# Attention, feed-forward and gate in one kernel: exponentials without a bias pointer, a new opening, new shares between ScalarE and VectorE, last sums in halves

## The chip, the cores and the metric

The kernel runs on one core of a Trainium2 chip. Its engines are TensorE (PE, matmuls; PEld are its weight loads), VectorE (DVE), ScalarE (ACT), GpSimd (POOL) and SyncE (SP, which mostly issues DMAs). The metric is the device time of one execution in microseconds. Executions of one kernel mostly agree within about 0.5%. Ratios are the mean time of one kernel's runs over the mean time of the other's runs in the same rounds, so they are not quite the ratios of the medians quoted beside them.

## The reference, cut to what matters

```python
B, S, D = 1, 2048, 640 ; H = 32 ; Dh = 20 ; F = 1536          # x, weights bfloat16
# A: attention without a mask
qkv = split(x @ wqkv)                       # per head q, k, v: 2048 x 20
p   = softmax(q @ k.T * Dh ** -0.5)         # 32 heads x 2048 x 2048 exponentials
a   = concat(p @ v) @ wo
# B: feed-forward with mish
h   = x @ w1 + b1
b   = (h * tanh(log1p(exp(h)))) @ w2
g   = sigmoid((x * gate_w).sum(-1))
out = g * a + (1 - g) * b
```

There are 134 million exponentials. ScalarE looks them up. The kernel gives a part of them to VectorE, which builds the bits of an approximate exponential by arithmetic.

## The kernel before

The work is cut into 32 groups G: four heads (one of eight sets `p`) by 512 queries. In a group there are 16 key tiles of 128 keys. Each key tile goes to ScalarE or to VectorE.

- ScalarE's key tiles: TensorE fills S0 or S1 (two banks of PSUM each) with the scores of two heads, 128 keys by 2 x 512 queries. One ScalarE instruction makes the exponentials of 128x1024 into an exp buffer E in SBUF. Two of these are one key tile for four heads.
- VectorE's key tiles: scores go to D. VectorE converts them to 16-bit integers that are the bits of a bfloat16 exponential (t0), and makes two shifted copies (t1, t2). The sum of the three is the approximation, too large by the constant 3.1187. So ScalarE's exponentials were made too large by the same constant, through the bias ln(3.1187), and the normalisation takes it out of both.
- X is one more bank, for the projections and the feed-forward.
- TensorE multiplies the buffers by the values into C, one single bank of PSUM. A group's sums must be complete, and copied from C by VectorE (`oraw`), before the next group may start in C. Until then the exp buffers of the next group can't be freed. There are six.

A scheduler written into the kernel, in Python, decides the order of every engine's instructions before the program is built. It goes by a cost that each task is given, and by starting points (`at(...)`, in groups) of the projections and of the feed-forward stages, which are fitted between the attention's work. It also inserts junk matmuls ("filler", line 378 of before) into TensorE's expected gaps, to hold its clock.

```python
DVE_KEYS = (1, 4, 7, 10, 13, 14)
MISH_IN = (4, 10, 11, 17, 24, 25)
def dve_keys(G):                       # VectorE's key tiles of group G: 152 of 512 in all
    if G == 0:
        return DVE_KEYS[2:5]
    return DVE_KEYS[:6 if G in MISH_IN else 4 + G % 2]
# ...
        def ex(sb=sb, eb=eb, w=w):     # ScalarE: exponentials of two heads
            eb.tile = epool.tile([P, 2 * QC], BF16, tag="E", name="E")
            nc.scalar.activation(eb.tile[:, 0:w * QC], sb.tile[:, 0:w * QC], ACT.Exp, bias=lnc, scale=inv)
        te.__init__("ACT", 143 + 0.833 * w * QC, ex, [ts, prev], ...)      # cost told to the scheduler, ns
# ...
            def p1(xb=xb, hp=hp):      # VectorE: the bits of the exponentials
                nc.vector.tensor_scalar(out=bufs[0].tile[...], in0=xb.tile,
                    scalar1=P * LOG2E * inv, scalar2=127.0 * P, op0=ALU.mult, op1=ALU.add)
# ...
    for c in range(NQ):                # the feed-forward's starting points
        base = 0.9 + 6.6 * c
        for ft in range(FT):
            h_unit(c, ft, at(base + 2.8 * ft / FT), base)
        mish(c, base + 3.1)            # Exp, Ln, Tanh on ScalarE, 128x2048 from SBUF to SBUF
```

The softmax here doesn't subtract the row's maximum and nothing guards it: scores larger than these inputs give would overflow.

Of the kernel before, what the change touches and what calls it, by code (L numbers as in the profile page):

```python
# [10 lines left out]
P = 128  # L11
# [25 lines left out]

def dve_keys(G):
    if G == 0:
        return DVE_KEYS[2:5]  # L40
    return DVE_KEYS[:6 if G in MISH_IN else 4 + G % 2]

# [7 lines left out]
MISH_IN = (4, 10, 11, 17, 24, 25)  # L50
# [8 lines left out]
class Task:  # L59
    def __init__(self, eng, cost, fn, deps=(), after=None, prio=5, rings=(),  # L60
                 frees=(), lat=70, mode=None, rows=(), key=0, port=False, work=0):
        self.eng, self.cost, self.fn = eng, cost, fn
        self.deps, self.after, self.prio = [d for d in deps if d], after, prio
        self.rings, self.frees = list(rings), list(frees)
        self.lat, self.mode, self.rows, self.key, self.port = lat, mode, rows, key, port
        self.start = self.end = self.before = None

        self.work = work or {"row": 128 * len(rows), "col": 2.4 * cost - 15, "full": 2.2 * cost}.get(mode, 0)


class Ring:
    def __init__(self, n):
        self.free = deque((0.0, s) for s in range(n))

# [9 lines left out]
class Order:  # L84
# [4 lines left out]
    LOW = 2  # L89
    WARM = 0.55  # L90
# [38 lines left out]
    def pick_pe(self, c):  # L129
# [19 lines left out]
        if X and X[1].due + 14 < self.visit:  # L149
            lim = min(lim, X[0])  # L150
            over = min(over, lim + self.OVER)
        ok = []
        for e, t in rest:
            if self.units and t.rings and t.rings[0].unit:
                continue
            if e <= now + 1 and e + self.cost(t) <= over and lim > now + 1:
                ok.append((e, t))
        if ok:
            short = self.spare and len(self.spare.free) < self.LOW
            return min(ok, key=lambda x: (  # L160
                x[1].prio - (1.2 if x[1].mode == self.mode else 0)
                - (1 if short and x[1].prio == 2 else 0), x[1].key, x[1].n))
# [39 lines left out]
    def run(self):  # L202
# [16 lines left out]
        while left:  # L219
# [42 lines left out]
            for b in t.rings:  # L262
                b.slot = b.ring.free.popleft()[1]
            for b in t.frees:
                b.users -= 1
                b.last = max(b.last, t.end)
                if b.users == 0:
                    b.ring.free = deque(sorted(list(b.ring.free) + [(b.last, b.slot)]))
                    if b.unit:
                        self.units -= 1  # L270
# [16 lines left out]
def kernel(  # L287
# [35 lines left out]
    pair = const.tile([P, 2], F32, tag="pair")  # L323
    lnc, mask = pair[:, 0:1], pair[:, 1:2]
    oc = const.tile([P, NQ * 4 * QC], BF16, tag="oc")
    bs = const.tile([P, 3 * NU * D], BF16, tag="bs")
    arena = const.tile([P, 2 * FT * QC], BF16, tag="arena")
# [20 lines left out]
    def bs_of(c):  # L348
# [5 lines left out]
    epool = ctx.enter_context(tc.tile_pool(name="epool", bufs=6))  # L354
# [8 lines left out]
    R = {k: Ring(n) for k, n in (  # L363
        ("S0", 1), ("S1", 1), ("X", 1), ("D", 1), ("E", 6), ("T0", TB[0]), ("T1", TB[1]), ("T2", TB[2]),
# [26 lines left out]

    nc.vector.memset(gw, 0.0)
    nc.vector.memset(lnc, log(SUM))
# [15 lines left out]
    ld_x = {0: [load_x(nc.scalar, 0, 2, 4000), load_x(nc.sync, 2, 4, 4000)]}  # L409
# [22 lines left out]
    def warm():  # L432
        junk.tile = pt(junk)
        for i in range(20):
            nc.tensor.matmul(junk.tile[:, 0:P], lhsT=ident, rhs=ident, start=True, stop=True)
    t_warm = o.add("PE", 2500, warm, [t_ident], prio=1.05, mode="full", rings=[junk], frees=[junk])
# [4 lines left out]
    for c in range(4):  # L441
        for i, kts in enumerate(((0, 1), (2, 3), (4,))):
            w = len(kts)
            buf = Buf(R[("D", "S0", "S1")[i] if c == 0 else "XD"[(c + i) % 2]])
# [9 lines left out]
            on_act = c == 0 and i == 1  # L454

            def ev(c=c, kts=kts, buf=buf, on_act=on_act):
                dst = xt[:, c, kts[0]:kts[0] + len(kts), :]
                src = buf.tile[:, 0:512 * len(kts)].rearrange("p (k q) -> p k q", q=QC)
                if on_act:
                    nc.scalar.copy(out=dst, in_=src)  # L460
                else:
                    nc.vector.tensor_copy(out=dst, in_=src)
            t_xt[c, i] = o.add("ACT" if on_act else "DVE",
                               160 + 0.833 * 512 * w if on_act else from_psum(512 * w, 0.52),
                               ev, [t], prio=1, key=c, frees=[buf])
    xt_of = lambda c: [t_xt[c, 0], t_xt[c, 1], t_xt[c, 2]]


    def unit(n, cost, mm, evac, ev_cost, deps, after, key, prio=3, ev_prio=2, eng="DVE", takes=(),
             ev_deps=(), ev_frees=(), mode="col", ring="X"):  # L470
# [3 lines left out]
        for k in range(n):  # L474
            def fn(k=k):
                if k == 0:
# [4 lines left out]
                         rings=[buf] if k == 0 else [], mode=mode, key=key)  # L481
        return o.add(eng, ev_cost, lambda: evac(buf.tile), [prev] + list(ev_deps), prio=ev_prio, key=key,
# [19 lines left out]
    first_of = {}  # L502
    for n, blk in enumerate(passes):
        for r, G, j in blk:
            first_of.setdefault(G, n)
    first_of[NG] = len(passes)
# [11 lines left out]
    def k_unit(p, sc, after, prio=3, key=0, ring="X"):  # L518
        if sc == 0:
            k_buf[p] = Buf(R["K"])  # L520

        def mm(t, k):
            for r in range(4):
                c = (4 * p + r) * DH
                w = w0[:, 1, k, r * DH:r * DH + 32] if p == 0 else wqk[:, k, D + c:D + c + 32]
                nc.tensor.matmul(t[32 * r:32 * r + 32, 0:QC], lhsT=w, rhs=xt[:, sc, k, :],  # L526
                                 start=k == 0, stop=k == KT - 1, tile_position=(0, 32 * r))
        t_k[p, sc] = unit(
            KT, 219, mm,
            lambda t: nc.vector.tensor_scalar(  # L530
                out=kt[:, (p % 2) * S + sc * QC:(p % 2) * S + (sc + 1) * QC], in0=t[:, 0:QC],
                scalar1=mask, scalar2=None, op0=ALU.mult),
            746, xt_of(sc) + [ld_w0[1] if p == 0 else ld_wqk], after, key, prio,
            takes=[k_buf[p]] if sc == 0 else [], ring=ring)

    def q_unit(G, after, prio=3, key=0, ring="X"):
# [10 lines left out]
        def evac(t):  # L547
# [3 lines left out]
            else:  # L551
# [3 lines left out]
                      ring=ring)  # L555
# [30 lines left out]
    k_unit(0, 0, None, prio=1.1)  # L586
    q_unit(0, None, prio=1.1, ring="D")
# [54 lines left out]
    for p, a, z in ((1, 0.7, 2.8), (2, 4.0, 5.2), (3, 10.2, 11.2), (4, 12.6, 15.0), (5, 17.2, 18.4),  # L642
                    (6, 20.4, 23.0), (7, 24.1, 25.2)):
        for sc in range(4):
            k_unit(p, sc, at(a + (z - a) * sc / 4), prio=2.5, key=a + (z - a) * sc / 4)
    for b, a in ((1, 4.0), (2, 10.6), (3, 17.2)):
# [3 lines left out]
    t_sel = o.add("POOL", 2000, make_sel, [t_k[7, sc] for sc in range(4)], prio=2)  # L650
# [7 lines left out]
    def pv_four(G, items, term=0):  # L658
# [4 lines left out]
        def fn():  # L663
# [3 lines left out]
            for r, (j, _, buf, off) in enumerate(items):  # L667
# [5 lines left out]
                                 rhs=buf.tile.bitcast(BF16)[:, off * QC:(off + 1) * QC],  # L673
# [17 lines left out]
    for n, blk in enumerate(passes):  # L691
# [8 lines left out]
        deps = [t_q[G] for _, G, _ in blk] + [t_k[G // NQ, j // 4] for _, G, j in blk] + [ps]  # L700
# [6 lines left out]
        def ex(sb=sb, eb=eb, w=w):  # L707
            eb.tile = epool.tile([P, 2 * QC], BF16, tag="E", name="E")
            nc.scalar.activation(eb.tile[:, 0:w * QC], sb.tile[:, 0:w * QC], ACT.Exp, bias=lnc, scale=inv)  # L709

        te = marks[n]
        te.__init__("ACT", 143 + 0.833 * w * QC, ex, [ts, prev], prio=2, key=n, rings=[eb], frees=[sb])
# [10 lines left out]
    def d_batch(key):  # L723
# [6 lines left out]
        for hp in range(2):  # L730
# [6 lines left out]
            d = o.add("PE", 228, dfill, [go, t_q[G], t_k[G // NQ, j // 4]], prio=1, rings=[xb], mode="row",  # L737
# [3 lines left out]
            def p1(xb=xb, hp=hp):  # L741
                if bufs[0].tile is None:
# [3 lines left out]
                    scalar1=P * LOG2E * inv, scalar2=127.0 * P, op0=ALU.mult, op1=ALU.add)  # L746
# [32 lines left out]
    for G in range(NG):  # L779
# [7 lines left out]
        last = G == NG - 1  # L787

        def evac(G=G, ob=ob):
            ob.tile = opool.tile([P, QC], F32, tag="oraw", name="oraw")  # L790
            nc.vector.tensor_copy(out=ob.tile, in_=acc[G])  # L791
        t0 = o.add("DVE", from_psum(QC), evac, pv_done[G], prio=0, key=G, rings=[ob])

        if last:

            def spread_pe(ob=ob, den=den):
                den["p"] = psum.tile([P, QC], F32, tag="C", name="Cd")
                nc.tensor.matmul(den["p"][:, :], lhsT=sel, rhs=ob.tile, start=True, stop=True)
            t1 = o.add("PE", 900, spread_pe, [t0, t_sel], prio=1.5, key=G, mode="full")

            def inverse(rb=rb, den=den):
                rb.tile = opool.tile([P, QC], F32, tag="rbc", name="rbc")
                nc.scalar.activation(rb.tile, den["p"], ACT.Ln)
                nc.scalar.activation(rb.tile, rb.tile, ACT.Exp, scale=-1.0)
            o.add("ACT", 1300, lambda: nc.scalar.preload_act_table_set("natural_log_exp_and_others"),
                  [prev], prio=1, key=G)
            t4 = o.add("ACT", 1180, inverse, [t1], prio=2, key=G, rings=[rb])
# [4 lines left out]
        if not last:  # L812
            t1 = o.add("SP", 2200, gather, [t0], prio=0, key=G)
# [4 lines left out]
        if not last:  # L818
            t2 = o.add("DVE", 245, rec, [t1], prio=2, key=G)
# [4 lines left out]
        if not last:  # L824
            t3 = o.add("SP", 2200, spread, [t2], prio=0, key=G)
# [5 lines left out]
        if not last:  # L831
            t4 = o.add("SP", 3000, bcast, [t3], prio=0, key=G, rings=[rb])
# [38 lines left out]
    def mish(c, group):  # L871

        done = []
        for i, func in enumerate((ACT.Exp, ACT.Ln, ACT.Tanh)):
            now = []
            for a in range(3):
# [11 lines left out]
                now.append(o.add("ACT", 1930 + (1300 if i and a == 0 else 0), fn, deps,  # L888
# [49 lines left out]

    def f_pair(c, u, ring, after):
# [3 lines left out]
        for k in range(6):  # L943
            for hf in range(2):
# [5 lines left out]
                prev = o.add("PE", 138, fn, deps + ([t_on[4 * NP - 4 + c][1]] if k == 5 else []), after=after,  # L950
# [8 lines left out]
    for c in range(NQ):  # L959
        base = 0.9 + 6.6 * c  # L960
        for ft in range(FT):
            h_unit(c, ft, at(base + 2.8 * ft / FT), base)
        mish(c, base + 3.1)
        for u in range(NU):
            for hf in range(2):
                b_unit(c, u, hf, at(base + 4.6 + 2.0 * (2 * u + hf) / 8), base + 4)
    PAIRS = ((2, ("D",) * 4, 32), (3, ("S0", "S1", "D", "S0"), 32))
    for c in range(2):
        for u in range(NU):
            for hf in range(2):  # L970
                f_unit(c, u, hf, at(29.3 + c + 0.6 * (2 * u + hf) / 8), 29 + c)
# [35 lines left out]
```

## Time and profile before

The median was 856.27 us (855.61 to 856.63).

| ScalarE before | us |
|---|---|
| span of the profiled run | 857.3 |
| busy | 812.7 |
| start of the first exponential | 12.5 |
| idle between the first and the last | 19.8 |
| from the end of the last to the end | 17.7 |

The first two lines are the busy time of each engine from the page, with its share of the span and the number of instructions, and ScalarE's row of the 40 slices (tenths of busy time).

```profile
PE 819.6 (96%) x10778; PEld 299.5 (35%) x10778; DVE 737.9 (86%) x981; ACT 812.7 (95%) x771; POOL 7.0 (1%) x10
...
ACT  4888999999999999999999999999999989999992
```

ScalarE is full nearly everywhere; TensorE looks as full, but its record counts modelled ends and filler. The next lines are groups of instructions of before: line, engine, operation, what it writes and reads, shapes, count, then busy time in us and mean duration in ns, then idle time before it and who ended most of it.

```profile
L709 ACT ACTIVATE E<-S,pair 128x1024 bf16<-128x1024 f32 x720 | 734.8, 1138 | 20.0 <-PE C L670 10.9
L744 DVE TENSOR_SCALAR t<-D 128x1024 uint16<-128x1024 f32 x304 | 371.2, 1221 | 58.6 <-PE D L683 52.1
...
L881 ACT ACTIVATE arena<-arena 128x2048 bf16<-128x2048 bf16 x36 | 69.1, 1927 | 0.2
...
L378 PE MATMUL C<-xt,gw 128*32 128x512 bf16 (+6 forms) x476 | 35.1, 361 | 0.0
```

720 exponentials of 1138 ns would be 819 us, but their busy time is 735: neighbours overlap. So a duration is not what one more costs; the distance from start to start is. The table of windows, for the exponentials alone (length of the stretch, busy time, count, granted clock, DMA share, GB/s), shows a full stretch:

```profile
518.00:614.00 96.00, 95.73 (x96) 1.00 0.06 17
```

For activations without a pointer there are the feed-forward's, three of 128x2048 in a row, in the chain of waits of before (start, length, what):

```profile
681.19 5.51 ACT arena L881 x3
```

Last, who kept ScalarE waiting before (total us, times, longest):

```profile
ACT E L709 <- PE C L670: 10.9, 8, 3.1
ACT E L709 <- PE S L683: 5.2, 8, 2.7
```

This profile is of an execution that took 859.09 us, 2.8 more than the median. Its clock record has half clock from 690.0 to 696.8 us, and ScalarE is idle for 2.3 us between 690 and 697. So some of the 19.8 us of idle time may belong to this execution and not to the kernel.

### The profile page before, as it was taken

The page shows a single profiled execution, that of the slowest core. Times are in us where ns is not written, and L with a number is a line of the kernel's source. Part 1 is how long each engine was busy: PE and PEld are TensorE (multiplying, and loading weights), DVE is VectorE, ACT ScalarE, POOL GpSimd, SP SyncE. Part 2 cuts the span into 40 slices and gives each one's busy share as a digit, 9 for nine tenths or more (in the row PEclk, how much of TensorE's full clock was granted, in tenths as well). Part 3 has the DMA queues.
Part 4 walks back from the last instruction along what each step waited for, and adds up shares of the span by engine and source line. Part 5 has one row for each costly group of instructions (what it writes and reads, how often), then busy time and mean ns, then how long its engine had stood idle before and what let it go on. Part 6 is the DMA issues. An engine that isn't in the chain of part 4 may idle for free.

```text
span 857.3 us, 24774 instructions
## 1 busy us (share of the span) xinstructions
PE 819.6 (96%) x10778; PEld 299.5 (35%) x10778; DVE 737.9 (86%) x981; ACT 812.7 (95%) x771; POOL 7.0 (1%) x10
## 2 busy tenths in 40 slices
PE   8999999899999998999999999999999999999998
PEld 5422234333323343333322333333223333333335
DVE  3699999998889999999898978889898988978984
ACT  4888999999999999999999999999999989999992
POOL 2000000000000000000000000000000000000000
PEclk9999999999999999999999999999999989999999
DMA  9510000000000000000000000000000000000112
GB/s 320 152 17 17 12 12 19 15 15 11 19 18 18 18 15 5 19 19 19 19 19 18 15 5 18 18 16 18 19 6 18 19 2 19 19 19 23 37 38 72
DMA packets 32244, 25.23 MB, mean 29 GB/s; under 512 B 17731, under 2 KB 26883, under 8 KB 32135
## 3 DMA queue, kind: packets, MB, share of 16 engines
q1 hardware_dynamic: 30678, 22.55, 9.2%
q8 instruction: 84, 1.38, 0.7%
q10 hardware_dynamic: 1456, 1.10, 0.4%
q14 instruction: 26, 0.20, 0.1%
HBM read 18.20 MB, written 2.88 MB: 25 GB/s over the span
## 4 chain that ended last, share of the span: by engine, by line
PE 54%; ACT 30%; issue 9%; DVE 5%; DMA 2%; SPq 0%; DVEq 0%; ACTq 0%
ACT E L709 26%; PE S L683 16%; PE C L670 14%; PE X L488 11%; PE D L683 4%; ACT arena L881 3%; DVE t L744 3%; PE X L526 3%; PE X L544 2%; PE X L564 1%; PE D L488 1%; PE C L378 1%; DMA rows<-rec 1%; PE S L488 1%; DMA rbc<-rows 1%
## 5 line engine op out<-in xcount | busy, mean ns | idle before, releaser
L709 ACT ACTIVATE E<-S,pair 128x1024 bf16<-128x1024 f32 x720 | 734.8, 1138 | 20.0 <-PE C L670 10.9
L744 DVE TENSOR_SCALAR t<-D 128x1024 uint16<-128x1024 f32 x304 | 371.2, 1221 | 58.6 <-PE D L683 52.1
L683 PE MATMUL S<-q,kt 32*128 32x512 bf16 x1440 | 279.3, 383 | 18.3 <-ACT E L709 14.4
L758 DVE TENSOR_SCALAR t<-t 128x2048 uint16<-128x2048 uint16 x304 | 199.9, 682 | 1.4 <-PE C L670 0.3
L683 PEld LDWEIGHTS <-kt 32*128 32x128 bf16 x2048 | 91.5, 91 | 289.3 <-issue 276.5
L670 PE MATMUL C<-E,va 128*32 128x512 bf16 x1440 | 142.4, 388 | 1.4 <-DVE oraw L791 1.3
L683 PE MATMUL D<-q,kt 32*128 32x512 bf16 x608 | 118.1, 383 | 6.7 <-DVE t L744 5.3
L670 PE MATMUL C<-t,vs 128*32 128x512 bf16 x1216 | 112.6, 384 | 1.0 <-DVE t L758 1.0
L670 PEld LDWEIGHTS <-va 128*32 128x32 bf16 x2048 | 54.5, 95 | 85.9 <-issue 71.6
L488 PE MATMUL X<-w,arena 128*32 128x320 bf16 x1536 | 80.4, 306 | 0.0
L488 PE MATMUL X<-xt,w 128*32 128x512 bf16 x960 | 73.7, 383 | 1.0 <-DVE arena L867 0.7
L881 ACT ACTIVATE arena<-arena 128x2048 bf16<-128x2048 bf16 x36 | 69.1, 1927 | 0.2
L670 PE MATMUL C<-t,va 128*32 128x512 bf16 x608 | 61.7, 383 | 1.0 <-DVE oraw L791 0.5
L488 PEld LDWEIGHTS <-arena 128*32 128x32 bf16 x1536 | 33.9, 96 | 35.6 <-issue 27.7
L670 PEld LDWEIGHTS <-vs 128*32 128x32 bf16 x1216 | 31.3, 95 | 36.6 <-issue 27.6
L544 PE MATMUL X<-xt,wqk 128*32 128x512 bf16 x560 | 42.5, 382 | 0.0
L526 PE MATMUL X<-xt,wqk 128*32 128x512 bf16 x560 | 41.5, 382 | 0.0
L867 DVE TENSOR_SCALAR arena<-X,b 128x512 bf16<-128x512 f32 x48 | 35.7, 743 | 3.0 <-PE X L488 2.8
L378 PE MATMUL C<-xt,gw 128*32 128x512 bf16 (+6 forms) x476 | 35.1, 361 | 0.0
L488 PEld LDWEIGHTS <-w 128*32 128x32 bf16 x960 | 21.2, 95 | 30.4 <-issue 22.5
L564 PE MATMUL X<-wvt,xt 128*128 128x160 bf16 x310 | 28.3, 233 | 1.4 <-DVE kt L530 0.7
L530 DVE TENSOR_SCALAR kt<-X,pair 128x512 bf16<-128x512 f32 x30 | 22.4, 746 | 8.3 <-PE X L526 8.2
(82 smaller groups left out, 335.3 us busy)
## 6 DMA issues: line engine op xcount, KB each, us to landing
rbc<-rows SPq DMA_DIRECT2D x124, 64.0 KB
w<-in_B_w_dram SPq DMA_DIRECT2D x2, 1920.0 KB
out_dram<-arena SPq DMA_DIRECT2D x16, 160.0 KB
oc<-on SPq DMA_DIRECT2D x96, 20.0 KB
wqk<-in_A_wqkv_dram SPq DMA_DIRECT2D x1, 1600.0 KB
arena<-in_A_x_dram SPq DMA_DIRECT2D x2, 640.0 KB
wvt<-in_A_wqkv_dram SPq DMA_DIRECT2D x1, 800.0 KB
arena<-in_A_x_dram ACTq DMA_DIRECT2D x1, 640.0 KB
```

The source lines that it names most:

```text
L378: nc.tensor.matmul(t[32 * r:32 * r + 32, 0:n], lhsT=gw[:, 0, 1:33], rhs=xt[:, r, 0, 0:n], start=G is None, stop=G is None, tile_position=( ...
L488: nc.tensor.matmul(t[32 * r:32 * r + 32, 0:width], lhsT=lhsT(r), rhs=rhs, start=a, stop=b, tile_position=(0, 32 * r))
L526: nc.tensor.matmul(t[32 * r:32 * r + 32, 0:QC], lhsT=w, rhs=xt[:, sc, k, :], start=k == 0, stop=k == KT - 1, tile_position=(0, 32 * r))
L544: nc.tensor.matmul(t[32 * r:32 * r + 32, 0:QC], lhsT=w, rhs=xt[:, qc, k, :], start=k == 0, stop=k == KT - 1, tile_position=(0, 32 * r))
L564: nc.tensor.matmul(t[:, n * 160:(n + 1) * 160], lhsT=xt[:, js[n] // 4, k, (js[n] % 4) * P:(js[n] % 4 + 1) * P], rhs=wv[:, k, 160 * b:160 * ...
L670: nc.tensor.matmul(acc[G][32 * r:32 * r + 32, :], lhsT=vs4[:, b, term - 1, DVE_KEYS.index(j), h:h + 32] if term else va4[:, b, j, h:h + 32 ...
L683: nc.tensor.matmul(t[:, off * QC:(off + 1) * QC], lhsT=kt[32 * r:32 * r + 32, (p % 2) * S + j * P:(p % 2) * S + (j + 1) * P], rhs=q_buf[G] ...
L709: nc.scalar.activation(eb.tile[:, 0:w * QC], sb.tile[:, 0:w * QC], ACT.Exp, bias=lnc, scale=inv)
L744: nc.vector.tensor_scalar(out=bufs[0].tile[:, 2 * QC * hp:2 * QC * (hp + 1)], in0=xb.tile, scalar1=P * LOG2E * inv, scalar2=127.0 * P, op0 ...
L758: (nc.vector if eng == "DVE" else nc.gpsimd).tensor_scalar(out=bufs[i].tile[:, a * w:(a + 1) * w], in0=bufs[0].tile[:, a * w:(a + 1) * w], ...
L867: lambda t: nc.vector.tensor_scalar(out=hs[:, ft, :], in0=t[:, 0:QC], scalar1=b1[:, ft:ft + 1], scalar2=None, op0=ALU.add),
L881: nc.scalar.activation(v, hs[:, 4 * a:4 * a + 4, :] if i == 0 else v, func, bias=1.0 if i == 1 else 0.0)
```

## The change

The intent: make each of ScalarE's exponentials shorter by not reading a bias from memory, start them earlier, and refit everything else to the faster ScalarE.

1. The constant 3.1187 moves from ScalarE's bias into VectorE's additive constant, where it is free. The scheduler is told 95 ns above 0.833 ns per column instead of 143 (and 1805 for the feed-forward's activations instead of 1930, whose instructions do not change).
2. The first 512 tokens come by four loads of 128, are transposed one by one, and Q goes first, then K for 128 keys alone, so that the first scores can start early. Seven spare exp buffers, in memory that the feed-forward needs only later, serve the first 48 exponentials.
3. VectorE's share is listed group by group: 143 key tiles instead of 152. The starting points of projections and feed-forward are set anew. The scheduler may pull a projection forward that is needed within 12 steps.
4. The last group's sums are copied, inverted and normalised in two halves of 256 queries.

```diff
-def dve_keys(G):
-    if G == 0:
-        return DVE_KEYS[2:5]
-    return DVE_KEYS[:6 if G in MISH_IN else 4 + G % 2]
+SHARE = (3, 3, 4, 5, 4, 6, 5, 3, 5, 3, 6, 5, 4, 4, 5, 4, 5, 4, 6, 4, 5, 4, 4, 5, 5, 5, 5, 5, 3, 5, 5, 4)
+DENSE = (1.55, 6.9, 12.8, 19.3)
+MISH = (1.15, 3.1, 2.15, 2.45)
+DOWN = (4.1, 3.45, 3.75, 4.45)
+KEYS = ((1, 0.8, 2.65), (2, 3.4, 5.65), (3, 11.25, 11.8), ...)
+def dve_keys(G):
+    n = SHARE[G]
+    return DVE_KEYS[2:2 + n] if G == 0 else DVE_KEYS[:n]
 ...
-        ("S0", 1), ("S1", 1), ("X", 1), ("D", 1), ("E", 6), ...
+        ("S0", 1), ("S1", 1), ("X", 1), ("D", 1), ("E", (13, 6, 48)), ...
 ...
-            eb.tile = epool.tile([P, 2 * QC], BF16, tag="E", name="E")
-            nc.scalar.activation(eb.tile[:, 0:w * QC], sb.tile[:, 0:w * QC], ACT.Exp, bias=lnc, scale=inv)
+            a, i = (es, eb.slot) if eb.slot < 6 else (bs, eb.slot - 6)
+            eb.tile = a[:, i * 2 * QC:(i + 1) * 2 * QC]
+            nc.scalar.activation(eb.tile[:, 0:w * QC], sb.tile[:, 0:w * QC], ACT.Exp, scale=inv)
 ...
-        te.__init__("ACT", 143 + 0.833 * w * QC, ex, [ts, prev], ...)
+        te.__init__("ACT", 95 + 0.833 * w * QC, ex, [ts, prev], ...)
 ...
-                    scalar1=P * LOG2E * inv, scalar2=127.0 * P, op0=ALU.mult, op1=ALU.add)
+                    scalar1=P * LOG2E * inv, scalar2=P * (127 - log2(SUM)), op0=ALU.mult, op1=ALU.add)
 ...
-    k_unit(0, 0, None, prio=1.1)
-    q_unit(0, None, prio=1.1, ring="D")
+    q_unit(0, None, prio=1.1, ring="S0")
+    k_unit(0, 0, None, prio=1.1, key=0.1, ring="S1", hi=P)
+    k_unit(0, 0, None, prio=1.1, key=0.2, ring="D", lo=P)
```

## The prediction

> **What bounds the kernel now.** ScalarE, in the middle. The page's first part has it busy 812.7 us of 857.3 (95%), 734.8 of that in 720 exponentials of 128x1024. The table of windows shows it full where no opening or tail disturbs it: 95.7 of 96 us from 518 to 614 us, with 96 exps, so 0.997 us each; VectorE is at about 89% there. TensorE's 98% counts modelled ends and 119 groups of junk matmuls that fill its gaps (35.1 us in the groups). Counting its real work at 0.216 us per group of four, with about 0.10 us for each of the 1468 changes between row and column tiling, both spacings read from the timeline, I estimate 770 to 780 us: TensorE is second, at about 91%. ScalarE's other 44.6 us are idle: 12.5 before the first exp, about 10 in the opening (2.2 to 3.1 us gaps, most behind the matmuls that free exp buffers), about 16 after the last exp, the rest scattered.
>
> **The bias pointer.** An exp with it lasts 1129 ns (median) and follows its predecessor after 997. The Trainium skill, "ScalarE: Activation LUTs", section "What ACT_TABLE_LOAD costs", gives about 93 ns for a pointer operand and about 93 ns of overlap between neighbours. The trace has activations without one: 597 ns for 512 columns, 1912 for 2048, and three of 2048 in 5.51 us, so 1.80 us apart, 94 ns above 0.833 per column. Estimate for the new exp: about 1035 ns long, but 947 ns apart. Only 50 of the 93 ns are worth anything, since the pointer's time was partly overlapped. The factor 3.1187 moves into VectorE's additive constant, free.
>
> **Shares.** The sum falls from 152 to 143 key tiles: 18 exps more (+17 us of ScalarE), 18 fewer VectorE conversions (1.22 us) and 18 fewer shifts (0.66 us): VectorE 738 to about 704 us; TensorE loses 18 groups of matmuls, about 4 us. Net ScalarE: 738 at 947 against 720 at 997 is 19 us less; busy falls to about 793.
>
> **Opening.** First score after Q and 128 tokens of K, not 512: first exp at about 10.5 us instead of 12.5. Thirteen exp buffers instead of six remove most of the idle behind matmuls in the first 90 us: 5 to 7 us.
>
> **Tail.** Halved sums take 0.5 to 1 us off the path from last exp to last normalisation, but the chain of waits has TensorE from 842 to 853.8 us without a break: at most 1 us.
>
> **Sum.** 856.3 - 19 - 2 - 6 - 1 = 828. Regrouping of shares, keys and feed-forward stages should fill some scattered gaps; against it TensorE comes to about 93% and will make ScalarE wait a little more. I predict 827 us, 80% range 815 to 840; faster by over 2% 0.90, within 2% 0.09, slower 0.01.
>
> **What would show it.** Exp duration near 1035 ns and spacing 945 to 955 in full stretches; ScalarE busy 785 to 800; VectorE about 705; first exp at 10 to 11 us; gaps of exps behind PV matmuls before 90 us gone; the last exp to the end 15 to 16.5 us.
>
> **What would make it wrong.** The exp's spacing staying near 997 (pointer wholly hidden: then about 845). TensorE, not ScalarE, setting the pace: exps waiting on scores by 20 us or more, spacing in stretches clearly above 950 with idle in front (then 835 to 845). The granted clock falling where the filler is thinner (it has 101 groups left of 119). Or the opening's gaps being TensorE's backlog, so that more buffers only postpone the same matmuls; then the 6 us are lost. If the tuning closes the scattered gaps better than I credit, 815 to 820.

## The result, and the profile after

The changed kernel took 813.37 us (813.02 to 813.71), against 856.27 before: a ratio of 0.950 (95% interval 0.9483 to 0.9516). The prediction said 827, with a range from 815 to 840. It is faster as predicted, and by more than the range allowed. These are the lines that answer to those of before:

```profile
PE 776.3 (96%) x10642; PEld 281.7 (35%) x10642; DVE 706.3 (87%) x949; ACT 774.0 (95%) x791; POOL 6.6 (1%) x10
...
ACT  5899999999999999999999999999999999999991
...
L744 ACT ACTIVATE es<-S 128x1024 bf16<-128x1024 f32 x708 | 666.5, 1033 | 13.2 <-PE C L703 4.6
L779 DVE TENSOR_SCALAR t<-D 128x1024 uint16<-128x1024 f32 x286 | 349.2, 1221 | 52.1 <-PE D L716 48.5
...
L933 ACT ACTIVATE arena<-arena 128x2048 bf16<-128x2048 bf16 x36 | 68.0, 1911 | 0.3
...
L744 ACT ACTIVATE bs<-S 128x1024 bf16<-128x1024 f32 x30 | 29.7, 1031 | 0.8 <-PE S L716 0.6
...
L399 PE MATMUL C<-xt,gw 128*32 128x512 bf16 (+4 forms) x396 | 28.1, 359 | 0.0
```

The exponentials stand in two groups now, by their buffers (es, and the spare ones in bs): 738 in all. Their busy times, 666.5 and 29.7 us, can't be added, because neighbours of different groups overlap; by their records they cover 692.9 us together, so 939 ns each. Before it was 734.8 / 720 = 1021. Their mean duration of 1033 ns is what the prediction had (1035), yet the busy time is not. ScalarE's busy time fell by 38.7 us, from 812.7 to 774.0, where the prediction had 19. Its idle time fell from 44.6 to 37.1 us, by 7.5, where the prediction had 9. So nearly all that was missed lies in the busy time. (The span fell by 46.2 us in these two profiles, the medians by 42.9: the profiled execution of before was a slow one, as said.) The feed-forward's activations (line 881 before, 933 after) did not change.

From the starts of the records, the median distance between two exponentials in a row is 0.996 us before and 0.920 after; after, nearly half of them lie at 0.903 or 0.904. The 18 additional exponentials show in VectorE's column (286 conversions for 304; VectorE is busy 706.3 us, predicted 705).

The waits of ScalarE after:

```profile
ACT es L744 <- PE C L703: 4.6, 5, 3.4
ACT es L744 <- PE S L716: 3.9, 10, 1.6
```

Waits behind exp buffers (PE C frees them) fell from 10.9 to 4.6 us, and waits for scores did not grow: the loss that the prediction feared, to TensorE as the next limit, did not come. The first exponential starts at 10.31 us (predicted 10 to 11, before 12.48). The end got longer, not shorter: 19.3 us from the last exponential to the end of the span, 17.7 before. The last exponential ends at 839.58 before and at 791.88 after. These are the chains of waits of before and after around those times, in both of which TensorE does the final matmuls (L488 before, L517 after) until 853.76 and 807.44, nearly without a break (the longest after is 0.2 us):

```profile
838.89 0.82 PE D L488 x24
839.71 0.32 PE C L670 x4
840.02 0.82 PE D L488 x24
840.84 1.09 PE Cd L798 x2
```

```profile
791.89 0.65 PE C L703 x9
792.54 0.68 PE D L517 x20
793.22 1.08 PE X L837 x4
```

Before, 24 of the 384 final matmuls of the last 1024 tokens (D) were done ahead of the last products (C x4), while ScalarE was still at its last exponential. After, none was; and 12 matmuls of the last group's products were left instead of 4 (the chain shows nine of them). That is 0.82 us for the 24 in D, and 0.65 us in C against 0.32: some 1.15 of the 1.38 us by which TensorE's run from there is longer (15.56 for 14.18). The halves did not shorten the path either: the last normalisation ended 4.4 us after the last exponential before (843.95), and 4.45 us after (796.33).

### The profile page after: what moved, and what is told of

Same layout as the page of the kernel before. It is cut to its first block, busy times and chain, and to the rows that moved or that the text cites. A ratio compares the mean times of both kernels' runs of the same rounds, so it can differ in the third digit from the quotient of the medians.

```text
span 811.1 us, 24412 instructions
## 1 busy us (share of the span) xinstructions
PE 776.3 (96%) x10642; PEld 281.7 (35%) x10642; DVE 706.3 (87%) x949; ACT 774.0 (95%) x791; POOL 6.6 (1%) x10
## 4 chain that ended last, share of the span: by engine, by line
PE 58%; ACT 33%; DVE 4%; issue 4%; DMA 1%; ACTq 0%; DVEq 0%
ACT es L744 23%; PE S L716 19%; PE C L703 17%; PE X L517 11%; ACT arena L933 7%; PE X L577 3%; PE X L557 3%; DVE t L779 2%; PE X L597 1%; ACT bs L744 1%; PE D L517 1%; DMA wvt<-in_A_wqkv_dram 1%; PE D L716 1%; ACT L933 1%; PE C L399 1%
## 5 line engine op out<-in xcount | busy, mean ns | idle before, releaser
L744 ACT ACTIVATE es<-S 128x1024 bf16<-128x1024 f32 x708 | 666.5, 1033 | 13.2 <-PE C L703 4.6
L779 DVE TENSOR_SCALAR t<-D 128x1024 uint16<-128x1024 f32 x286 | 349.2, 1221 | 52.1 <-PE D L716 48.5
L716 PE MATMUL S<-q,kt 32*128 32x512 bf16 x1476 | 285.9, 384 | 15.7 <-ACT es L744 12.1
L793 DVE TENSOR_SCALAR t<-t 128x2048 uint16<-128x2048 uint16 x286 | 190.2, 681 | 1.3
L716 PEld LDWEIGHTS <-kt 32*128 32x128 bf16 x2048 | 80.5, 91 | 273.7 <-issue 263.5
L703 PE MATMUL C<-es,va 128*32 128x512 bf16 x1416 | 140.6, 385 | 1.3 <-DVE oraw L826 1.2
L716 PE MATMUL D<-q,kt 32*128 32x512 bf16 x572 | 111.3, 385 | 4.1 <-DVE t L779 3.5
L703 PE MATMUL C<-t,vs 128*32 128x512 bf16 x1144 | 106.3, 383 | 0.3 <-DVE t L793 0.2
L517 PE MATMUL X<-w,arena 128*32 128x320 bf16 x1536 | 82.0, 305 | 0.1
L517 PE MATMUL X<-xt,w 128*32 128x512 bf16 x960 | 72.3, 383 | 2.5 <-DVE arena L919 1.4
L517 PEld LDWEIGHTS <-arena 128*32 128x32 bf16 x1536 | 33.4, 96 | 33.5 <-issue 26.4
L577 PE MATMUL X<-xt,wqk 128*32 128x512 bf16 x560 | 43.8, 383 | 0.0
L517 PEld LDWEIGHTS <-w 128*32 128x32 bf16 x960 | 22.7, 95 | 30.6 <-issue 22.7
L744 ACT ACTIVATE bs<-S 128x1024 bf16<-128x1024 f32 x30 | 29.7, 1031 | 0.8 <-PE S L716 0.6
L399 PE MATMUL C<-xt,gw 128*32 128x512 bf16 (+4 forms) x396 | 28.1, 359 | 0.0
```

The costliest lines, as they stand in the source:

```text
L399: nc.tensor.matmul(t[32 * r:32 * r + 32, 0:n], lhsT=gw[:, 0, 1:33], rhs=xt[:, r, 0, 0:n], start=G is None, stop=G is None, tile_position=( ...
L517: nc.tensor.matmul(t[32 * r:32 * r + 32, 0:width], lhsT=lhsT(r), rhs=rhs, start=a, stop=b, tile_position=(0, 32 * r))
L577: nc.tensor.matmul(t[32 * r:32 * r + 32, 0:QC], lhsT=w, rhs=xt[:, qc, k, :], start=k == 0, stop=k == KT - 1, tile_position=(0, 32 * r))
L703: nc.tensor.matmul(acc[G][32 * r:32 * r + 32, :], lhsT=vs4[:, b, term - 1, DVE_KEYS.index(j), h:h + 32] if term else va4[:, b, j, h:h + 32 ...
L716: nc.tensor.matmul(t[:, off * QC:(off + 1) * QC], lhsT=kt[32 * r:32 * r + 32, (p % 2) * S + j * P:(p % 2) * S + (j + 1) * P], rhs=q_buf[G] ...
L779: nc.vector.tensor_scalar(out=bufs[0].tile[:, 2 * QC * hp:2 * QC * (hp + 1)], in0=xb.tile, scalar1=P * LOG2E * inv, scalar2=P * (127 - log ...
```

## The experiments

Theory A, formed on this result: the pointer's share of the distance between exponentials was mis-sized. Rival B: it is worth the predicted 50 ns, and the rest came from the fixed exp buffers or the new order. "Order kept" below means that a comparison of the programs showed every engine's instructions in the same sequence; the traces agree. Every run gave correct results, except the one that was wrong on purpose. In the kernels with new orders, the second half of the last sums was made to follow the first, without which some could not be built; put into the changed kernel, this left its order as it is, by comparison of the programs (no run shows it).

### 1. The pointer alone, in both orders, and exponentials alone

Before, without the pointer; order kept:

```diff
-            nc.scalar.activation(..., ACT.Exp, bias=lnc, scale=inv)
+            nc.scalar.activation(..., ACT.Exp, scale=inv)
-                    scalar1=P * LOG2E * inv, scalar2=127.0 * P, ...
+                    scalar1=P * LOG2E * inv, scalar2=P * (127 - log2(SUM)), ...
```

> The kernel before with the bias pointer taken off its 720 exps and the factor moved into VectorE's constant; every engine's order is that of before. Theory A (the pointer's share of the exp's spacing was mis-sized in the prediction): exps follow each other after 0.90 to 0.92 us instead of 0.997, ScalarE's exps take 670 to 685 us instead of 735, and the time falls well below what the prediction's 50 ns would give, to 815 to 830 us. Rival B (the pointer is worth the predicted 50 ns, and the rest of the changed kernel's shorter spacing comes from its fixed exp buffers or its new order): spacing near 0.947, time 835 to 842 us.

After, with the pointer again (the reverse diff); order kept:

> The changed kernel with the bias pointer put back on its 738 exps and the factor back in the bias; every engine's order is that of the changed kernel. Theory A: spacing back to about 0.996 us, ScalarE busy up by 50 to 57 us, time 860 to 868 us, slower than the kernel before because it has 18 exps more. Rival B: spacing 0.95 to 0.96, time 840 to 850 us.

Nothing but activations, back to back:

```python
for n in range(12): nc.scalar.activation(o(n),      ps, ACT.Exp, bias=bias, scale=0.25)           # L92  PSUM, pointer
for n in range(12): nc.scalar.activation(o(12 + n), ps, ACT.Exp, scale=0.25)                      # L94  PSUM
for n in range(12): nc.scalar.activation(o(24 + n), src[:, 0:1024], ACT.Exp, bias=bias, scale=0.25)  # L96 SBUF, pointer
for n in range(12): nc.scalar.activation(o(36 + n), src[:, 0:1024], ACT.Exp, scale=0.25)          # L98  SBUF
for n in range(6):  nc.scalar.activation(o2(n),     src, ACT.Exp, scale=0.25)                     # L100 SBUF, 2048
for n in range(12): nc.scalar.activation(ping[n % 2], ps, ACT.Exp, bias=bias, scale=0.25)         # L102 waits on its own engine
for n in range(12): nc.scalar.activation(ping[n % 2], ps, ACT.Exp, scale=0.25)                    # L104
```

> Only ScalarE at work, a wrong result on purpose: series of 12 exps of 128x1024 back to back, from PSUM and from SBUF, with and without the pointer, and 6 of 128x2048 from SBUF without; then the two PSUM series again, each writing over the output of two before, as a wait on its own engine. Theory A: from PSUM 0.995 us with the pointer and 0.904 to 0.920 without; from SBUF without it 0.947, as the feed-forward activations had it (0.094 above 0.833 ns per column), so the prediction took its overhead from the wrong memory. Rival B: 0.947 without the pointer from both memories. If the waits on its own engine cost the 16 ns that tell 0.904 from 0.920 in the changed kernel, the last two series show it.

The timeline of that last kernel, ScalarE only (start, length of the series, line, count):

```profile
2.70 12.16 ACT L92 ACTIVATE outs<-ps,bias 128x1024 bf16<-128x1024 f32 x12
14.66 11.17 ACT L94 ACTIVATE outs<-ps 128x1024 bf16<-128x1024 f32 x12
25.51 12.74 ACT L96 ACTIVATE outs<-src,bias 128x1024 bf16<-128x1024 bf16 x12
37.97 11.61 ACT L98 ACTIVATE outs<-src 128x1024 bf16<-128x1024 bf16 x12
49.32 11.05 ACT L100 ACTIVATE outs<-src 128x2048 bf16<-128x2048 bf16 x6
60.11 12.31 ACT L102 ACTIVATE ping<-ps,bias 128x1024 bf16<-128x1024 f32 x12
72.07 11.32 ACT L104 ACTIVATE ping<-ps 128x1024 bf16<-128x1024 f32 x12
```

The start of each series less the start of the one before, over its count, is the distance: from PSUM (14.66 - 2.70) / 12 = 0.997 us with the pointer and 0.904 without; from SBUF 1.038 and 0.946; 2048 columns from SBUF 1.798. So the pointer costs 92 or 93 ns from either memory, and none of it is hidden by the neighbours. Reading from PSUM is 42 ns cheaper per instruction than reading from SBUF. Above 0.833 ns per column (853 ns for 1024; the two lengths from SBUF give (1798 - 946) / 1024 = 0.832) that is 51 ns from PSUM and 93 from SBUF. In these series the type differs with the memory, float32 in PSUM and bfloat16 in SBUF. Against the type speak the durations of the last sums, which are float32 throughout and have no pointer (a logarithm reads PSUM, an exponential SBUF): 597 ns from PSUM and 630 from SBUF for 512 columns before (L803, L804), 376 and 417 on average for 256 after (L842, L843). No series parts memory from type. Waits on ScalarE's own earlier work, long done, cost nothing (the last two series have the distances of the first two, 0.997 and 0.904). Rival B falls, and the prediction's mistake has its place: it took the overhead of the feed-forward's activations, which read SBUF, for exponentials that read PSUM.

In the kernels: without the pointer, the kernel before had a median distance of 0.921 us; with it, the changed kernel had 0.997. Why the median without it is 0.920 in the full kernel and 0.904 alone stays open; it is not the wait on its own engine, which the last series had too.

The times are less simple. The changed kernel with the pointer took 857.2 us (ratio to before 1.0005, 0.999 to 1.002): put back, the pointer costs 43.8 us, 59 ns for each of 738. All the rest of the change, with the pointer left in and in this order, is worth nothing on balance; it includes 18 exponentials more. But the pointer alone, taken off the kernel before, gave 836.9 us (0.977, 0.9755 to 0.9784): only 19.6 us. The exponentials' group of that run, from its page, and then ScalarE's waits in it:

```profile
L709 ACT ACTIVATE E<-S 128x1024 bf16<-128x1024 f32 x720 | 689.2, 1028 | 43.1 <-PE S L683 22.6
```

```profile
ACT E L709 <- PE S L683: 22.6, 70, 2.7
ACT E L709 <- PE C L670: 12.1, 8, 3.2
```

The exponentials take 45.6 us less than before (689.2 for 734.8; theory A had expected 670 to 685), but ScalarE's idle time between the first and the last exponential grows from 19.8 to 42.9 us. It waits for scores in 70 places. The old order was made for slower exponentials. Both times miss what theory A expected (815 to 830 and 860 to 868 us), and 836.9 even lies in the range of rival B. So the times do not decide between them; the distances do, 0.921 and 0.997 in the kernels and 0.904 alone, where B had 0.947.

### 2. A new order for faster exponentials, alone

```diff
-        te.__init__("ACT", 143 + 0.833 * w * QC, ex, [ts, prev], ...)
+        te.__init__("ACT", 95 + 0.833 * w * QC, ex, [ts, prev], ...)
```

on top of the kernel before without the pointer; the scheduler makes the order anew.

> As the first of these, but the kernel's own scheduler is told 48 ns less per exp, so it orders the work anew for faster exps; nothing else of the change. Theory A: 812 to 825 us, a few us under the run with the old order. Rival B: about 835 us.

It took 845.4 us (0.988), 8.5 us more than with the old order. Both theories missed this. Idle time between the exponentials is 59.5 us, in gaps of up to 9.1 us. So a truer cost does not by itself give a better order, and something else must be in the way.

### 3. One part of the change taken back: shares, starting points

```diff
-    n = SHARE[G]
+    n = 3 if G == 0 else 6 if G in (4, 10, 11, 17, 24, 25) else 4 + G % 2
```

> The changed kernel with VectorE's shares as before (152 key tiles instead of 143, six in the six groups of the old feed-forward places, four and five in turn elsewhere). If the shares are what lets the shorter exp pay: ScalarE has 18 exps less (about 16 us of work) and yet the time rises, to 820 to 835 us, with ScalarE idle more behind scores and VectorE at 90%. If ScalarE's work alone sets the pace: about 798 to 805 us.

```diff
-DENSE = (1.55, 6.9, 12.8, 19.3) ; MISH = (1.15, 3.1, 2.15, 2.45) ; DOWN = ... ; KEYS = ... ; VALUES = ... ; OUT = ...
+DENSE = (0.9, 7.5, 14.1, 20.7) ; MISH = (3.1,) * 4 ; DOWN = (4.6,) * 4 ; # and the old points of KEYS, VALUES, OUT
```

> The changed kernel with the old starting points of the projections and the feed-forward stages, which were set for slower exps. If the starting points are what lets the shorter exp pay: 825 to 845 us, with ScalarE waiting for the feed-forward sums or for scores late. If not: 813 to 818.

The old starting points cost 4.7 us (818.1 us, 0.955). The old shares cost everything: 856.2 us (0.9997, 0.998 to 1.001), well above the 820 to 835 expected, and the waits are for exp buffers and not for scores. ScalarE was busy 755.6 us, 18 less than in the changed kernel, and idle 72 us between the exponentials, 64 of them in twelve gaps over 1 us. All these gaps carry the same name in the table of waits:

```profile
ACT es L744 <- PE C L703: 65.5, 14, 11.5
```

But TensorE was not the cause. Here is the longest but one, on three engines: ScalarE, then VectorE, then TensorE, from the timelines (start, length, line, what, idle time before it).

```profile
329.66 6.53 ACT L744 ACTIVATE es<-S 128x1024 bf16<-128x1024 f32 x7
346.78 1.94 ACT L744 ACTIVATE es<-S 128x1024 bf16<-128x1024 f32 x2 [10.59 <-PE C L703]
```

```profile
341.40 1.23 DVE L779 TENSOR_SCALAR t<-D 128x1024 uint16<-128x1024 f32 x1 [0.33 <-PE D L716]
342.55 0.54 DVE L956 TENSOR_SCALAR bs<-X,g 128x320 bf16<-128x320 f32 x1
343.11 1.23 DVE L779 TENSOR_SCALAR t<-D 128x1024 uint16<-128x1024 f32 x1
344.25 0.68 DVE L793 TENSOR_SCALAR t<-t 128x2048 uint16<-128x2048 uint16 x1
345.00 0.55 DVE L956 TENSOR_SCALAR bs<-X,g 128x320 bf16<-128x320 f32 x1
345.47 0.68 DVE L826 COPY oraw<-C 128x512 f32<-128x512 f32 x1
```

```profile
344.99 0.40 PE L703 MATMUL C<-t,vs 128*32 128x512 bf16 x4
...
346.30 0.39 PE L703 MATMUL C<-es,va 128*32 128x512 bf16 x4
```

ScalarE stops at 336.2, with its six buffers full of the next group's exponentials. VectorE works nearly without a pause: it still has conversions of the old group to do (779), then their shift (793), and sums of the feed-forward in between (956). Only then can TensorE multiply the last shifted part into C (344.99), VectorE empty C (826, at 345.47), and TensorE take the first of the next group's exponentials (346.30), which frees a buffer. ScalarE goes on at 346.78. The wait is put down to PE C, which came last; the chain behind it is VectorE's lateness in the old group.

### 4. The fit of shares and starting points

The kernel with the old shares had also moved the feed-forward away from the groups with six. So both parts were taken back together, and, in another kernel, the total of 143 was spread evenly:

```diff
+SHARE = (3, 4, 5, 4, 5, 4, 5, 4, 5, 4, 5, 4, 5, 4, 5, 4, 5, 4, 5, 4, 5, 4, 5, 4, 5, 4, 5, 4, 5, 4, 5, 5)
```

> The changed kernel with both the old shares and the old starting points, which were set for one another; exps still without the pointer, opening, spare buffers and halves still new. The run with old shares alone lost everything (856 us), but its shares of six stand in groups from which the new starting points have moved the feed-forward's ScalarE work. If that mismatch is what cost it: 828 to 845 us here, with gaps behind exp buffers fewer than its 65 us. If fewer key tiles for VectorE (143 for 152) is what matters whatever their place: about 850 us again.

> The changed kernel with the same total of 143 key tiles for VectorE, but spread evenly, four and five in turn. All engines have the same total work as in the changed kernel. If the total is what matters: 813 to 818 us. If it is the fit of each group's share to what else VectorE and ScalarE have in that group: 825 to 845 us, with gaps of several us in which ScalarE waits for an exp buffer at the ends of groups where VectorE is late.

With both old: 846.6 us (0.988), between the two expectations, idle 63.1 us between the exponentials. That is the 845.4 us of experiment 2: with the old shares and starting points, the new opening, the spare buffers and the halves gave nothing that shows. Spread evenly: 827.5 us (826.5 to 834.2; the profiled run, with a span of 832.3, was one of the slower ones), idle 30.0 us, 7.0 of them in one gap behind VectorE's sums of the feed-forward and 13.6 in waits for scores, where gaps behind exp buffers had been expected.

### 5. The exp buffers of the opening

Six buffers throughout, `("E", 6)`:

> The changed kernel with six exp buffers throughout instead of thirteen for the first 48 exps. The prediction credited the spare ones with 5 to 7 us. If they only postpone TensorE's backlog: 813 to 816 us. If they are worth what was predicted: 818 to 821 us with ScalarE waiting for exp buffers 7 to 12 us before 90 us.

Four more than the change has, in memory that is free until the ninth group, `("E", (17, 6, 48))`; this was meant to be faster:

> The changed kernel with four more spare exp buffers at the start, in the part of the output projection's input that stays unused until the ninth group; an attempt at a faster version. The changed kernel still has one gap of 3.4 us behind an exp buffer at 27 us. If ScalarE's start is what holds: 810 to 812 us. If TensorE has the backlog to do anyway: 813 to 815, with waits for scores in place of the gap.

Six buffers took 827.2 us (0.965; 825.0 to 831.2), with waits behind exp buffers of 20.2 us (4.6 in the changed kernel), some of them at 209 and 724 us, far from the opening. Seventeen took 830.1 us (0.968): the gap at 30 us shrank from 3.4 to 1.8 us, and new ones came at 66, 201, 507 and 725 us. Neither matches what was expected. A change in the opening gives another order up to the end of the program. So the difference between two such kernels is not the worth of the part that differs.

### 6. Is the filler in the way?

The junk matmuls are left out, the order of everything else kept:

> The run of the kernel before without the pointer (836.9 us), now also without the junk matmuls that fill TensorE's gaps (480, 35 us of busy records, about 26 us at 0.216 us per four); every other instruction stands in the same order. If TensorE with its filler is what took back about 25 us of the shorter exps: 815 to 825 us, scores waited for less. If the old order itself is at fault: 832 to 837. If the filler was holding the clock: granted clock below 0.98 and no gain.

> The changed kernel without its 404 junk matmuls, all else in the same order. If filler costs nothing where ScalarE sets the pace: 812 to 814 us, and if the clock holds perhaps 1 to 4 us less; a fall of the granted clock would show as a slower run.

Both got slower: 848.5 us for 836.9 (0.991 of before), 821.6 for 813.4 (0.959). The granted clock of the whole run fell from 1.0 to 0.966 and from 0.997 to 0.974. The row of the clock in the 40 slices, of the changed kernel and of the same without filler:

```profile
PEclk9999999999999999999999999999999999999999
```

```profile
PEclk9999999979999988999999999999999979999999
```

By the table of its waits, TensorE's longest in the changed kernel without filler was 2.5 us, another was 2.4, and all others were at most 1.6. In the other kernel without filler no break between matmul records was over 1.3 us. The clock record knows full and half clock only; in the changed kernel without filler, half clock comes in five stretches of 3.4 to 13.7 us before the end. So the filler pays. Whether TensorE's load would have allowed more in the old order can't be told from this run, because the clock changed with it.

### 7. How much is the order itself?

```diff
-        te.__init__("ACT", 95 + 0.833 * w * QC, ex, [ts, prev], ...)
+        te.__init__("ACT", 94 + 0.833 * w * QC, ex, [ts, prev], ...)      # and 96, and 67
```

> The changed kernel with one number of its scheduler's cost model 1 ns lower (94 for 95 above 0.833 ns per column). The work of every engine is the same, only the order is made anew. If the order of the changed kernel was picked as a lucky one among many: 820 to 832 us. If orders of this quality come by themselves: 812 to 815 us.

> The same, 1 ns higher. Together with the run 1 ns lower it gives the spread of orders: lucky order 820 to 832 us, otherwise 812 to 815 us.

> The changed kernel with its scheduler told the spacing that the trace has, 67 ns above 0.833 per column (0.920 us) for 95. If a true cost makes a better order: 805 to 812 us. If the shares and starting points are fitted to the number 95: 818 to 835 us, as with any other new order.

Nine key tiles more for VectorE, in groups that had four (2, 4, 12, 15, 17, 19, 21, 22 and 31):

> The changed kernel with nine key tiles more for VectorE, 152 as before, added to nine groups that had four, so that ScalarE has 18 exps less. If VectorE's total stalls ScalarE: 838 to 856 us, ScalarE waiting 40 us or more for exp buffers. If only the misplaced sixes of the old shares did it: 815 to 832 us, within the spread of the orders.

These show how much the order decides. One nanosecond in the scheduler's cost of an exponential, with the same work on every engine but for filler (404 junk matmuls in the changed kernel, 564 with 94, 648 with 96, 444 with 67), made 835.9 us (0.975) and 841.5 us (0.981) of 813.4; 67, which belongs to the median of 0.920, made 842.2 (0.981). All three are slower than either expectation. Their traces part from the changed kernel's first at 55, 37 and 14 us, far before the last sums, so it is not the fixed sequence of the halves. The number of junk matmuls does not follow the times either. Idle time between the exponentials was 34.7, 36.5 and 39.8 us instead of 13.0. The largest gap in the run with 96, 6.3 us at 505 us, has the same form as the one shown: VectorE's last shift and the last products, C emptied at 504.05, then the next group. With nine key tiles added it took 857.8 us (1.0005), with 66.2 us idle. Both are outside what the orders with 143 gave. But the number 152 does not by itself set the time: of the kernels without the pointer and with filler, five have 152 (836.9 to 857.8 us, 42.9 to 72.0 idle) and eight have 143 (813.4 to 842.2 us, 13.0 to 39.8 idle). The idle times keep apart, and the times overlap.

| kernel | us | ScalarE busy | idle between exponentials | last exponential to end |
|---|---|---|---|---|
| before | 856.3 | 812.7 | 19.8 | 17.7 |
| before without pointer | 836.9 | 767.4 | 42.9 | 18.1 |
| the same, new order | 845.4 | 756.6 | 59.5 | 21.0 |
| after with pointer | 857.2 | 825.5 | 5.8 | 19.3 |
| **after** | **813.4** | **774.0** | **13.0** | **19.3** |
| after, told 94 / 96 / 67 | 835.9 / 841.5 / 842.2 | 773.3 / 775.5 / 769.4 | 34.7 / 36.5 / 39.8 | 20.8 / 20.8 / 26.1 |
| after, 143 spread evenly | 827.5 | 775.9 | 30.0 | 21.2 |
| after, 152 shares (nine added) | 857.8 | 757.0 | 66.2 | 27.0 |
| after, old shares | 856.2 | 755.6 | 72.0 | 20.8 |
| after, old shares and points | 846.6 | 755.7 | 63.1 | 21.1 |

(Times are medians; busy and idle are of the profiled run.) Reading down: ScalarE's work, its idle time and what comes before and after the exponentials make the time. With 152 shares VectorE has about 737 us of work and ScalarE about 756 in the new orders. With 143 it is 706 against 774. That ScalarE must stop wherever a group gives VectorE a little more than its part is the likely reason; it was not tested group by group. Giving ScalarE 18 exponentials more, 17 us at 0.939, takes 26 to 32 us of idle time off in the orders made anew (66.2 to 34.7 and 39.8), and 53 in the chosen one.

## Why the prediction was wrong, point by point

- **The term that was mis-sized: the exponential's spacing.** The prediction put it as "738 at 947 against 720 at 997 is 19 us less". Measured by their busy time it is 738 at 939 against 720 at 1021, so 41.9 us less; by the median distance of starts, 920 ns for 947. (ScalarE's whole busy time fell by 38.7, since exponentials and other activations overlap less after.) The pointer is worth 92 to 93 ns back to back (76 at the medians in the kernel), not "only 50 of the 93", and none of it was overlapped. Both facts behind the 50 were right by themselves (0.997 with the pointer; 94 ns overhead in the feed-forward's activations). The mistake was to join them: they read different memories. The trace of before had the clue: of the two durations that the prediction quotes, 597 ns for 512 columns is a read from PSUM (L803) and 1912 for 2048 from SBUF, and above 0.833 ns per column they are 171 and 206 ns. With the 38.7 for 19 the prediction's own sum would have been 809. With 0.904 for every exponential it would have been 51 less for their term alone; the kernel's longer distances take back about 9 of that.
- **The skill's numbers.** The Trainium skill, "ScalarE: Activation LUTs", section "What ACT_TABLE_LOAD costs", says that each pointer operand adds about 93 ns. The series alone confirm it, 0.092 and 0.093 us. The prediction set this aside for its own subtraction, saying that the pointer's time "was partly overlapped". The same section's 186 ns less 93 of overlap gives, as an estimate, the 93 ns of overhead that SBUF showed; from PSUM it is 51.
- **Direction and limit were right.** ScalarE set the pace before and after: its busy time fell by 38.7 us, its idle time by 7.5, and the span by 46.2.
- **The idle terms nearly held in sum.** First exponential at 10.31 us (10.5 predicted), so 2.2 us earlier. Idle time between exponentials fell by 6.8 us (about 6 predicted for the opening). The waits behind exp buffers before 90 us, said to be gone, fell from 7.7 to 3.4 us. How much of this the spare buffers did alone stays open, since no kernel with another number of buffers keeps the order.
- **The tail was wrong.** Predicted were 15 to 16.5 us, measured 19.3 us; and the prediction's "about 16" for before was a misreading of 17.7. The path to the last normalisation did not shorten (4.4 and 4.45 us), and TensorE had more left to do.
- **The second limit was named wrongly.** The prediction had TensorE at 91 to 93% and feared its scores. What stops ScalarE in six of the slower kernels (old shares, both old, nine added, told 94, 96 and 67) is mostly an exp buffer: after 30 us they have 41 gaps over 2 us that carry the name PE C, 202 us in all, and VectorE was idle in 9 of these. So it is VectorE's lateness in the old group, as in the gap shown. It does not hold for every order: the kernel before without the pointer waits 22.6 us for scores and 12.1 for buffers, told the new cost 17.3 and 22.1 (and 14.5 for sums of the feed-forward), and with the shares spread evenly 13.6 and 3.6. There TensorE is not cleared. VectorE was at 86% of the span before, but its work has a deadline in every group.
- **What the prediction did not see:** that the gain of 43 us hangs on one order. Its sum took it for granted that the new order would leave ScalarE as little idle as the old one. The chosen order does (13.0 us). Others that the scheduler makes of nearly the same numbers leave 35 to 40 us, and with them the whole change is worth 14 to 20 us (836 to 842).

What stays open: why the exponentials have two distances, 0.904 and 0.920 us, in the full kernel; how much the opening's spare buffers and the starting points are worth by themselves, since their differences (14 and 5 us) lie within the spread of the orders (28 us); which property of the chosen order keeps ScalarE fed; and how much of the 42.9 us idle in the old order without the pointer was TensorE's load and how much its order. That the values of the change were found by trying many orders is a guess from their look; no run shows how they were made.

## What to carry to other kernels

Take the cost of an instruction in a full pipeline from the distance of starts, for the same source memory and the same operands, or measure it alone in a series: durations and subtractions between unlike instructions can be off by half. When a list scheduler places everything, change its cost by 1 ns first: the spread (28 us here) tells how large a difference must be before it says anything about a part of a change. When the wait at a shared accumulator names the engine that came last, follow it back through the group's last addend; the late engine can be one whose average load looks harmless.

## What the Trainium skill lacked or had wrong

- "ScalarE: Activation LUTs", section "What ACT_TABLE_LOAD costs": its numbers do not tell the source memory apart. Back to back and without a pointer, 1024 columns take 0.904 us from PSUM and 0.946 from SBUF (51 and 93 ns above 0.833 per column); with the pointer 0.997 and 1.038. The page's note that ScalarE is faster to PSUM is about the destination. The skill does have the difference, on another page: "Perfetto Trace Analysis", section "Optimizing Scalar/DVE Operations", gives an overhead of about 93 ns for ScalarE on SBUF and about 51 on PSUM, and the series agree with both. The prediction did not look there, and the first page does not point to it.
- "TensorE: Matmul & The Clock Gate", section "Why this matters for your kernels", asks for no idle gaps over about 3 us. Here the granted clock fell to 0.974 with no gap over 2.5 us and all but two at most 1.6, when the filler was taken out, and in the kernel before without pointer and filler to 0.966 with none over 1.3. The page's section "A second HAM failure mode: psum-queue depth-cycling" tells of short idle times that do this, but gives no number for how short.
- No page tells that a wait which ends with one engine's instruction may be another's lateness; the gap of 10.6 us shown above, named PE C, was VectorE's.
